# Scattering the transposed keys and queries over partitions in steps of three, in a scan-attention and mixture-of-experts kernel

## The chip, the cores and the metric

The kernel runs on one core of a Trainium2 chip. The time is the device time in microseconds (us) of one execution. Three runs of the kernel before took 1787.15, 1789.98 and 1791.46 us; the median is 1789.98 us. Durations of single instructions come from one profiled execution, which took 1786.6 us, of which 1784.6 us lie between its first and its last instruction (the span).

## The reference, cut to what matters

Four batches, eight heads, 768 time steps, 48 dimensions per head. A linear attention with a complex decay per key dimension, and on its output a layer of eight experts whose gates are balanced by eight rounds of row and column scaling.

```
for t in range(S):                                 # attention, per batch and head
    new_re = ar * S_re - ai * S_im
    new_im = ar * S_im + ai * S_re
    S_re, S_im = new_re + outer(k[t], v[t]), new_im
    y[t] = q[t] @ S_re                             # sums over the 48 key dimensions
x = y as [3072 tokens, 384]
P = exp(x @ w_gate - max), then 8 rounds of row and column scaling
for e in range(8):                                 # every expert on every token
    out += P[:, e:e+1] * (relu(x @ w1[e]) @ w2[e])
```

## The kernel before

The decay is turned into a running complex product z over time (`scan`), so that a block of time steps becomes matmuls: keys are divided by z (the tile `kh`, real and imaginary), queries are multiplied by it (in place in `zt`), and then scores, state and output are products over the key dimension. All matmuls of the experts run in fp32r with a high and a low part, so each product is three matmuls.

**First phase** (`phase1`, about the first 600 us). Twelve sub-blocks (`i` from 0 to 11) of 256 time steps each, three to a batch, each in two chunks of 128. For every sub-block: `load` (queries and keys, values), `norm` (decays, one sub-block ahead), `scan` and `post` on VectorE (DVE) with some steps on ScalarE (ACT), `attention`, `logits`, and, one sub-block later, the first two experts (`experts(i - 1)`), which are most of TensorE's (PE's) work. **Second phase** (`phase2a`, `phase2b`): the other six experts by a scheme that needs fewer products (15 for a 3 by 3 by 2 block), with weight sums prepared on VectorE, stored to DRAM (`w_d`) and fetched again for later blocks of tokens.

**Order of the work.** The program of the first phase is laid out by `Plan`: each step is a job with an engine, a cost, a rank, tiles that it reads and writes, and for a transfer the time `land` after which its result is expected (3.0 us for the transfers below, beside a cost of 0.68 us on SyncE's queue, SP). `order` runs the jobs through four in-order queues (PE, DVE, ACT, SP) and takes at each point the ready job of lowest rank; that order is then fixed in the program. The waits between engines are semaphores that the framework sets from which parts of a tile are written and read.

**The transfers in question** (lines 545 to 553). `scan` and `post` hold channels on 128 partitions: partition 8 d + h of channel third `ct` (0 to 2) is key dimension 16 ct + d of head h. The matmuls of attention want the key dimension on partitions and the head along the row. So twelve transfers per sub-block, from SBUF to SBUF, all issued from SP, re-lay them: `ks` (keys) and `qs` (queries) are tiles of 112 partitions, with real parts on rows 0 to 47 and imaginary ones on rows 64 to 111 (a = 0, 1; rows 48 to 63 stay zero). One transfer takes one third of the channels of one half: it reads 128 partitions and writes 16, in rows of 1 KB (two chunks; queries have one column more, the decay at the end, which `turn`, lines 616 to 619, copies to `rr` and `rn`). That is 6 transfers of 128 KB and 6 of 129 KB. In sub-block 0 (`i < THIRD`) the rank puts real and imaginary of a third side by side; in all others the three thirds of the real half go first.

**Who reads them.** PE: `keys` (line 574, transposes of `ks`), `scores` (line 588), `outs` (line 613). ACT: lines 617 and 618 (real column of `qs`), 619 (imaginary). DVE: line 649 (`sb`, for the new state), line 591 (masked scores). All depend on all of `ks` or all of `qs`. The experts' steps that run between them: lines 268 to 270 and 286 to 288 on PE, 274 on ACT, 278 on DVE (the low part `hl`).

**Memory.** Small constant tiles lie in the pool `cst`; the weights' pool `wp` comes directly behind it (ten tiles of 6144 bytes per partition, used in both phases), and the other pools of that side (`hp1`, `wx`, `wy`, `xp1`, later `hp2`, `ct`, `xc`, `xt`) behind `wp`. The tiles `qs`, `ks`, `zt`, `kh` and the second phase's X lie in pools allocated from the other end.

Of the kernel before, what the change touches and what calls it, by code (L numbers as in the profile page):

```python
# [6 lines left out]
F32 = mybir.dt.float32  # L7
# [13 lines left out]
NCH = SUB // CH  # L21
# [17 lines left out]
THIRD = 1  # L39
# [88 lines left out]
class Net:  # L128
# [9 lines left out]
    def build(self):  # L138
        tc, nc = self.tc, self.nc
        DR = bass.MemoryType.DRAM  # L140
        PS = bass.MemoryType.PSUM
        with ExitStack() as ctx:
            dram = ctx.enter_context(tc.tile_pool(name="dram", bufs=1, space=DR))
            cst = ctx.enter_context(tc.tile_pool(name="cst", bufs=1))
            self.wp = ctx.enter_context(tc.tile_pool(name="wp", bufs=WIDE))
            self.psA = ctx.enter_context(tc.tile_pool(name="psA", bufs=2, space=PS))

            self.ones = cst.tile([128, 128], F32, name="ones")
            nc.vector.memset(self.ones, 1.0)
            self.warm = cst.tile([128, 16], F32, name="warm")  # L150
            self.ident = cst.tile([128, 128], F32, name="ident")
            self.nident = cst.tile([128, 128], F32R, name="nident")
            self.mask = cst.tile([128, 4, CH], U8, name="mask")
            self.bm05 = cst.tile([128, 16], F32, name="bm05")
            nc.vector.memset(self.bm05, -0.5)
            self.bw = cst.tile([128, 16], F32, name="bw")
            nc.vector.memset(self.bw, -0.75 * 0.4995)
            self.wgs = cst.tile([128, NCT, 2 * E], F32R, name="wgs")
            self.two = cst.tile([2 * E, E], F32, name="two")
            self.wgr = cst.tile([128, NCT, E], F32, name="wgr")  # L160
            self.P = cst.tile([128, self.ntt, E], F32, name="P")

            ns = self.N // SUB
            self.fl = cst.tile([128, ns * (NCT * NCH + 2) + 2], F32, name="fl")
            self.ok = cst.tile([128, 9], F32, name="ok")
            self.oki = cst.tile([1, 1], mybir.dt.int32, name="oki")
            self.wt = {}
            self.x_d = [dram.tile([128, NS, 2, NCT, 2, CH], F32, name=f"x_d{u}") for u in range(self.N // UN)]
            self.ye_d = [[dram.tile([128, C], F32, name=f"ye_d{u}_{i}") for i in range(self.ntt) if u < 2 or i < NS * NCH] for u in range(E)]
            self.dram = dram  # L170

            with ExitStack() as c2, ExitStack() as cw, tc.manual_schedule(engines={mybir.EngineType.PE}):
                with ExitStack() as c1:
                    with ExitStack() as ca:
                        self.phase1(c1, ca)
                    self.phase2a(c2, cw)
                self.phase2b(c2, cw)
            flag = nc.values_load(self.oki[0:1, 0:1], min_val=0, max_val=1)
            with tc.If(flag < 1):
                with ExitStack() as c3:  # L180
                    self.general(c3)
# [345 lines left out]
    def attention(self, i):  # L527
        nc, V, A, job = self.nc, self.nc.vector, self.nc.scalar, self.plan.add
# [17 lines left out]
        for t, dst, src, w in (("ks", self.ks, kh, CH), ("qs", self.qs, zt, CH + 1)):  # L546
            for a in range(2):
                for ct in range(NCT):
                    p = 64 * a + 16 * ct
                    gs = range(ct * NCH, ct * NCH + NCH)  # L550
                    need = [("kh", a, g) for g in gs] + [("kr", a, g if i < THIRD else 0, k) for g in gs for k in range(TR)] if t == "ks" else [(*u, g) for u in (("z", s, a), ("ze", s)) for g in gs]
                    self.last = [job("SP", 0.68, lambda p=p, dst=dst, src=src, w=w, a=a, ct=ct: nc.sync.dma_start(dst[p:p + 16, :, :, :w], src[:, a, ct * NCH:ct * NCH + NCH, :w]),
                                     need, [(t, a, ct)], -3e6 + 40 * i + (2 * (t == "qs") + a + 4 * ct if i < THIRD else 6 * (t == "qs") + 3 * a + ct), land=3.0)]

        def chunk(c):
            ib = (i * NCH + c) % 2
# [845 lines left out]
```

## Time and profile before

| quantity | us |
|---|---|
| median of three runs | 1789.98 |
| profiled execution | 1786.6 |
| its span | 1784.6 |
| PE busy in the span | 1714.9 |
| DVE busy | 1285.6 |
| ACT busy | 805.2 |

A row of a table by stretches gives the stretch, then for PE, PE's weight loads (PEld), DVE, ACT and POOL the busy us with the count of instructions, then the granted clock of PE (1.00 is full speed), the mean busy share of the 16 DMA engines, and GB/s. In a list in time order a row is start, duration, engine, line, operation, output and inputs, and in brackets the idle time of the engine just before with what ended it. "Who waited for it" lists engine, line, idle us in total and how many times. The rows of transfers give their size in KB and the median us from issue to landing.

### The profile page before, as it was taken

How to read it: one execution, taken by the hardware profiler on the slowest of the kernel's cores; microseconds unless marked ns; L12 is line 12 of the kernel's file. 1: busy time of each engine (PE TensorE's matmuls, PEld its weight loads, DVE VectorE, ACT ScalarE, POOL GpSimd, SP SyncE). 2: the span in 40 equal slices, each digit the busy share in tenths (PEclk: the TensorE clock that was granted, in tenths of full speed). 3: DMA queues.
4: the chain of work that ended last, by engine and by line, in shares of the span. 5: the costliest groups of instructions: out<-in, count | busy, mean ns of one | idle time of the engine just before them, and what ended most of it. 6: DMA issues, size and time to landing. Idle time of an engine off the chain costs nothing.

```text
span 1784.6 us, 35158 instructions
## 1 busy us (share of the span) xinstructions
PE 1714.9 (96%) x13864; PEld 1664.0 (93%) x13864; DVE 1285.6 (72%) x2927; ACT 805.2 (45%) x1853; POOL 6.1 (0%) x13
## 2 busy tenths in 40 slices
PE   6899999999999889999999999999999999999998
PEld 3788899988898889999999999999999999999998
DVE  8788888888887468999884566766566765556564
ACT  7655555555554455565553433333333333333332
POOL 1000000000000000000000000000000000000000
PEclk9999999999999999999999999999999999999999
DMA  7455555555534675878896556576555657455561
GB/s 224 97 124 124 122 117 120 98 119 122 99 93 103 176 262 207 286 275 279 283 320 231 214 185 241 197 260 236 204 216 187 236 202 267 177 207 190 213 232 40
DMA packets 161422, 338.41 MB, mean 190 GB/s; under 512 B 13024, under 2 KB 120800, under 8 KB 161248
## 3 DMA queue, kind: packets, MB, share of 16 engines
q1 hardware_dynamic: 160448, 335.68, 59.0%
q8 instruction: 111, 1.82, 0.4%
q14 instruction: 63, 0.52, 0.1%
q10 hardware_dynamic: 800, 0.39, 0.1%
HBM read 236.07 MB, written 81.00 MB: 178 GB/s over the span
## 4 chain that ended last, share of the span: by engine, by line


## 5 line engine op out<-in xcount | busy, mean ns | idle before, releaser
L1137 ACT ACTIVATE hh<-s 128x384 fp32r<-128x384 f32 x384 | 201.9, 526 | 430.0 <-DVE s L1133 389.1
L1133 DVE TENSOR_TENSOR s<-s,A 128x384 f32<-128x384 f32 x316 | 174.4, 552 | 149.1 <-PE A L1119 145.6
L1042 PE MATMUL po<-w_d,hh 128*128 128x384 f32 x768 | 258.2, 336 | 0.0
L1041 PE MATMUL po<-w_d,hh 128*128 128x384 f32 x768 | 257.6, 335 | 0.0
L1043 PE MATMUL po<-w_d,hl 128*128 128x384 f32 x768 | 257.6, 335 | 0.0
L1144 DVE SCALAR_TENSOR_TENSOR hl<-s,hh 128x384 fp32r<-128x384 f32 x384 | 211.8, 552 | 6.2
L268 PE MATMUL ph<-xh,w 128*128 128x256 f32 x576 | 169.4, 294 | 1.6 <-ACT hf L274 1.2
L269 PE MATMUL ph<-xl,w 128*128 128x256 f32 x576 | 164.5, 286 | 0.0
L270 PE MATMUL ph<-xh,w 128*128 128x256 f32 x576 | 164.3, 285 | 0.0
L1130 ACT ACTIVATE s<-B 128x384 f32<-128x384 f32 x192 | 94.2, 491 | 121.9 <-PE B L1119 118.2
L1133 DVE TENSOR_TENSOR s<-s,B 128x384 f32<-128x384 f32 x189 | 104.1, 551 | 56.4 <-PE B L1119 54.3
L1042 PEld LDWEIGHTS po<-w_d,hh 128*128 128x128 f32 x768 | 144.3, 188 | 0.0
L1041 PEld LDWEIGHTS po<-w_d,hh 128*128 128x128 f32 x768 | 144.2, 188 | 0.0
L274 ACT ACTIVATE hh<-ph 128x256 fp32r<-128x256 f32 x192 | 73.5, 383 | 156.7 <-PE ph L270 153.6
L1043 PEld LDWEIGHTS po<-w_d,hl 128*128 128x128 f32 x768 | 144.2, 188 | 0.0
L286 PE MATMUL po<-w,hh 128*128 128x384 f32 x384 | 134.8, 351 | 0.4 <-ACT yst L294 0.4
L288 PE MATMUL po<-w,hl 128*128 128x384 f32 x384 | 131.7, 343 | 1.0 <-DVE hl L278 0.5
L287 PE MATMUL po<-w,hh 128*128 128x384 f32 x384 | 130.8, 341 | 0.0
L1042 PE MATMUL po<-w_c,hh 128*128 128x384 f32 x384 | 129.2, 336 | 0.0
L1041 PE MATMUL po<-w_c,hh 128*128 128x384 f32 x384 | 128.9, 336 | 0.0
L1043 PE MATMUL po<-w_c,hl 128*128 128x384 f32 x384 | 128.9, 336 | 0.0
L1152 DVE TENSOR_TENSOR s<-s,B 128x384 f32<-128x384 f32 x64 | 35.4, 554 | 119.2 <-PE B L1119 118.3
(248 smaller groups left out, 4109.6 us busy)
## 6 DMA issues: line engine op xcount, KB each, us to landing
w_d<-w_d SPq DMA_DIRECT2D x64, 768.0 KB, 7.2
w_a<-w_d SPq DMA_DIRECT2D x48, 768.0 KB, 4.3
w_b<-w_d SPq DMA_DIRECT2D x48, 768.0 KB, 5.7
w_c<-w_d SPq DMA_DIRECT2D x48, 768.0 KB, 6.5
raw<-in_w_dram SPq DMA_DIRECT2D x32, 576.0 KB, 5.3
w_d<-w_a SPq DMA_DIRECT2D x16, 768.0 KB, 3.3
w_d<-w_b SPq DMA_DIRECT2D x16, 768.0 KB, 4.7
w_d<-w_c SPq DMA_DIRECT2D x16, 768.0 KB, 6.1
```

The lines of the kernel that those rows point to most:

```text
L268: nc.tensor.matmul(p, w[:, 0, cs], xh[:, ct, :], start=(ct == 0), stop=False)
L269: nc.tensor.matmul(p, w[:, 0, cs], xl[:, ct, :], start=False, stop=False)
L270: nc.tensor.matmul(p, w[:, 1, cs], xh[:, ct, :], start=False, stop=(ct == NCT - 1))
L286: nc.tensor.matmul(o, hh[:, s], w2h, start=f == 0, stop=False)
L287: nc.tensor.matmul(o, hh[:, s], w2l, start=False, stop=False)
L288: nc.tensor.matmul(o, hl[:, s], w2h, start=False, stop=f == NF - 1)
L1041: nc.tensor.matmul(po[k], hh[:, s], w2[:, 0], start=c == 0, stop=False)
L1042: nc.tensor.matmul(po[k], hh[:, s], w2[:, 1], start=False, stop=False)
L1043: nc.tensor.matmul(po[k], hl[:, s], w2[:, 0], start=False, stop=c == NF - 1)
L1133: V.tensor_tensor(S[nm], S[nm], ps, op)
L1137: A.activation(hh, S[nm], AF.Relu)
L1144: V.scalar_tensor_tensor(hl, S[nm], 0.0, hh.bitcast(F32), ALU.max, ALU.subtract)
```

## The change

Three edits. A transfer of third `ct` starts at row 64 a + ct and writes every third row, so key dimension 16 ct + d goes to row 3 d + ct of its half in place of row 16 ct + d; keys and queries have the same new order, the 48 rows of a half are the same set. In sub-blocks 1 to 11 the rank puts real and imaginary transfers of one third in turn. A tile `gap` of 128 bytes per partition that nothing uses is put into `cst`, so that `wp`, and what lies behind it, begins 128 bytes later, at a multiple of 256 bytes.

```diff
             self.P = cst.tile([128, self.ntt, E], F32, name="P")
+            cst.tile([128, 32], F32, name="gap")
...
-                    p = 64 * a + 16 * ct
+                    p = 64 * a + ct
...
-                    self.last = [job("SP", 0.68, lambda p=p, dst=dst, src=src, w=w, a=a, ct=ct: nc.sync.dma_start(dst[p:p + 16, :, :, :w], src[:, a, ct * NCH:ct * NCH + NCH, :w]),
-                                     need, [(t, a, ct)], -3e6 + 40 * i + (2 * (t == "qs") + a + 4 * ct if i < THIRD else 6 * (t == "qs") + 3 * a + ct), land=3.0)]
+                    self.last = [job("SP", 0.68, lambda p=p, dst=dst, src=src, w=w, a=a, ct=ct: nc.sync.dma_start(dst[p:p + 3 * 15 + 1:3, :, :, :w], src[:, a, ct * NCH:ct * NCH + NCH, :w]),
+                                     need, [(t, a, ct)], -3e6 + 40 * i + (2 * (t == "qs") + a + 4 * ct if i < THIRD else 6 * (t == "qs") + 2 * ct + a), land=3.0)]
```

## The prediction

> **What bounds the kernel now.** I read the stages first (busy time per stretch of the span), then the idle time of TensorE and who caused it, then one sub-block closely on each queue, then the granted clock.
>
> ```profile
> span 1784.6 us, 35158 instructions
> PE 1714.9 (96%) x13864; PEld 1664.0 (93%) x13864; DVE 1285.6 (72%) x2927; ACT 805.2 (45%) x1853; POOL 6.1 (0%) x13
> ...
> core 0: us, PE busy (x) PEld busy (x) DVE busy (x) ACT busy (x) POOL busy (x), PEclk, DMA share, GB/s
> 450.00:500.00 50.00, 45.10 (x516) 42.64 (x516) 38.32 (x97) 25.49 (x70) 0.00 (x0) 0.93 0.52 107
> 1000.00:1200.00 200.00, 199.88 (x1138) 198.28 (x1137) 132.34 (x258) 71.20 (x141) 0.00 (x0) 1.00 0.60 220
> ```
>
> TensorE (PE) sets the time everywhere. In the second phase it is busy 199.88 of 200 us, so nothing that shortens a transfer or a VectorE step there can show. In the first phase (about the first 600 us, twelve sub-blocks of some 48 us) it is idle for several us in every 50, and its clock is at times below 1. The question is what those idle us wait for. The view of the line that issues the changed transfers, L552, answers it:
>
> ```profile
> L552 SPq DMA_DIRECT2D ks<-kh x72: 547/591/1305, 36.1 to 576.0; - x72
> L552 SPq DMA_DIRECT2D qs<-z x72: 547/597/1817, 37.6 to 579.9; - x72
> ...
>   DVE sb L649: 29.3, 11
>   ACT rn L619: 25.4, 12
>   PE s L588: 21.3, 11
> ...
>   PE s L574: 5.4, 7
> ...
> DMA to landing us min/median/max: 3.3/5.8/8.1
> ```
>
> Once per sub-block PE stands still for the queries (L588, the scores), 21.3 us in 11 waits, and seven times for the keys (L574), 5.4 us. VectorE and ScalarE stand still for the same transfers at the same time. So TensorE has no other work in its order while they travel, and this is on the path that sets the end. Sub-block 6, in time order on SP, PE, ACT and DVE:
>
> ```profile
> 327.09 3.79 SPq L552 DMA_DIRECT2D ks<-kh  x6
> 331.04 3.78 SPq L552 DMA_DIRECT2D qs<-z  x6
> ...
> 335.94 0.99 PE L574 MATMUL s<-ident,ks 112*128 112x112 f32 x8
> 342.31 1.33 PE L588 MATMUL s<-qs,ks 112*32 112x32 f32 x64 [2.25 <-DMA qs<-z]
> ...
> 339.27 0.22 ACT L617 ACTIVATE rr<-qs 48x8 f32<-48x8 f32 x1 [1.70 <-DMA qs<-z]
> 342.27 0.21 ACT L619 ACTIVATE rn<-qs 48x8 f32<-48x8 f32 x1 [2.56 <-DMA qs<-z]
> ...
> 342.29 0.56 DVE L649 TENSOR_TENSOR sb<-U,qs 48x384 f32<-48x384 f32 x1 [3.44 <-DMA qs<-z]
> ```
>
> The twelve transfers are issued within 7.7 us, 0.63 us apart (3.79 / 6). Yet the imaginary queries, which L619 reads, are there only at 342.27, 15.2 us after the first issue and some 7.5 us after the last one ended (331.04 + 3.78). The real ones (L617) were there at 339.27, 3.0 us earlier: the queue works them off one after another, slower than they are issued. PE arrived at 340.06 (342.31 - 2.25), 13.0 us after the first issue; VectorE at 338.85 (342.29 - 3.44), 11.8 us after. How fast the queue runs in that time:
>
> ```profile
> qs<-z SPq DMA_DIRECT2D x72, 129.0 KB, 7.1
> ks<-kh SPq DMA_DIRECT2D x72, 128.0 KB, 4.6
> ...
> 329.50:340.00 10.50, 10.49 (x133) 9.83 (x132) 9.04 (x26) 4.88 (x14) 0.00 (x0) 1.00 1.16 122
> 700.00:800.00 100.00, 99.99 (x570) 98.95 (x569) 92.90 (x253) 56.16 (x112) 0.00 (x0) 1.00 0.77 270
> ```
>
> The last two columns are the busy share of the DMA engines and what they moved. While the twelve travel, the engines are full (1.16, packets overlap) and move 122 GB/s, 105 per full share (122 / 1.16). In the second phase, where transfers write all 128 partitions, a full share is 351 GB/s (270 / 0.77). So it isn't the engines that are short, but what a transfer into 16 neighbouring partitions can take in.
>
> **The change part by part.** Step of three. It adds and removes no instruction: 144 transfers of the same bytes, and every consumer reads all 48 rows of a half, so a permutation of rows costs PE, ScalarE and VectorE nothing. What changes is the rate. The twelve hold 6 x 128 + 6 x 129 = 1542 KB, 1.58 MB; at 122 GB/s that is 12.9 us, and of the 15.2 us from first issue to use, 2.3 us are start and landing. For PE not to wait, the data may take 13.0 - 2.3 = 10.7 us, a rate of 148 GB/s; for VectorE not to wait, 11.8 - 2.3 = 9.5 us, 166 GB/s. The trace shows no destination with a step. The lower bound is the rate as it is, 122; the upper one is the issue, 129 KB in 0.63 us, about 208 GB/s, since 351 can't be fed. Between these I go by the spread of the destination: 16 rows give 105, 128 rows 351, so 46 rows, straight between them, about 171 GB/s (an estimate). That is above both thresholds: data 9.2 us, in use 11.5 us after the first issue, so PE's waits on queries and keys go: 21.3 + 5.4 = 26.7 us.
>
> [...]
>
> Order. Real and imaginary in turn adds nothing to issue. It lets the first imaginary keys go third or second where they went fourth, and SP might wait some tenths for VectorE to finish them; what is behind on SP (the queries, then stores of ye_d) isn't urgent, as the queue and not SP is late. In sub-block 0 the halves are issued in turn already:
>
> ```profile
> qs<-z SPq DMA_DIRECT2D x6, 129.0 KB, 5.6
> ```
>
> (the transfers by line in the first 50 us). 5.6 us there is better than the 7.1 of all, but those issues also lie further apart. I price the order alone at between 0 and the whole wait, and take 0, as the step already clears the thresholds. [...]
>
> Clock. When PE has stood still, its clock is halved for a while. These rows are the stretches of half clock after the waits, and one of full clock:
>
> ```profile
> 155.99:159.41 3.42, 3.42 (x15) 3.42 (x15) 1.79 (x5) 0.66 (x2) 0.00 (x0) 0.50 0.93 254
> 295.94:299.35 3.41, 3.41 (x15) 3.40 (x14) 2.69 (x8) 1.11 (x5) 0.00 (x0) 0.50 1.03 292
> 343.73:347.14 3.41, 3.41 (x14) 3.41 (x15) 2.97 (x8) 1.76 (x8) 0.00 (x0) 0.50 0.91 255
> 391.51:394.93 3.42, 3.36 (x69) 3.33 (x70) 2.72 (x5) 2.69 (x12) 0.00 (x0) 0.50 1.04 347
> 442.71:446.13 3.42, 3.42 (x17) 3.20 (x15) 2.48 (x8) 0.92 (x5) 0.00 (x0) 0.50 1.00 295
> 490.50:497.33 6.83, 4.62 (x39) 4.46 (x32) 4.13 (x13) 2.12 (x10) 0.00 (x0) 0.50 0.60 179
> 541.70:548.53 6.83, 6.16 (x77) 5.62 (x78) 4.46 (x11) 3.31 (x14) 0.00 (x0) 0.50 0.39 147
> 312.00:315.41 3.41, 3.41 (x24) 3.26 (x23) 3.38 (x7) 2.59 (x6) 0.00 (x0) 1.00 0.23 87
> ```
>
> 14 matmuls in 3.41 us against 24 at full clock. PE is busy 27.8 us in the seven rows together (3.42 + 3.41 + 3.41 + 3.36 + 3.42 + 4.62 + 6.16), half of which, 13.9 us, is lost to the clock. With the waits gone these should go. I keep back 3.4 us: two stretches of 3.4 us, half of each, for the two long rows, in which PE was also idle for other reasons.
>
> What is late next. VectorE is PE's partner in this phase:
>
> ```profile
> sum 480.00, PE 450.41 PEld 426.09 DVE 400.18 ACT 256.19 POOL 0.00; mean PE 45.04 PEld 42.61 DVE 40.02 ACT 25.62 POOL 0.00
> ...
> DVE hl L278 <- ACT hf L274: 34.1, 34, 2.7
> ```
>
> The first row is the sum of ten stretches of 48 us from 97 to 577, the second VectorE's longest waits from 50 to 640. Per sub-block VectorE works 40.0 us. PE works 45.0, of which 1.3 (13.9 / 11) is the clock, so 43.7: PE stays the longer one by 3.7 us, and VectorE's 34.1 us of waiting for PE's products (through ScalarE) is slack on PE's side. VectorE and ScalarE lose their own wait for the queries (29.3 and 25.4 us) with it. I keep back 1.2 us, 0.1 a sub-block, for new short waits of PE on VectorE.
>
> Gap. 128 bytes more ahead of the weights' pool: no instruction. It can only change the pace at which the pool's tiles are read or filled. Filling is hidden in the second phase (199.88 of 200). For reading, compare matmuls that stream from the pool with matmuls that stream from X, elsewhere, both 384 wide:
>
> ```profile
> L1041 PE MATMUL po<-w_d,hh 128*128 128x384 f32 x768 | 257.6, 335 | 0.0
> L1119 PE MATMUL B<-X,w_b 128*128 128x384 f32 x317 | 106.6, 336 | 0.0
> ```
>
> 335 and 336 ns: where the operand lies doesn't show. I take 0; rounding leaves half a ns either way, 7 us over 13,864 matmuls.
>
> The sum: 26.7 + 13.9 - 3.4 - 1.2 = 36.0 us off the profiled run's 1786.6 us (span 1784.6, 2.0 around it), so 1750.6. The median of the runs shown is 1789.98, 3.4 above the profiled run; from it, 1754.0.
>
> **The rivals.** VectorE binds. If the 34.1 us of waiting at L278 aren't slack but come back, VectorE can shed only its 29.3 us and PE waits at its products of hl: 1790 - 29 = 1761, worse if it waits for the later transfers too. For it: VectorE would be busy 40.0 of some 44 us, and the two are interlocked every 2 us. Against: those waits are VectorE waiting for PE, not the reverse.
>
> The rate doesn't move. If 122 GB/s is set by the reading side or by packets of 1 KB, the waits stay and so does the time, 1790. For it: in the same rows source and packets don't change either. Against: the reading side spans all 128 partitions, as in transfers that reach 351.
>
> The transfers wait for each other. The rows of the three thirds now interleave: each spans 46 rows that overlap the next one's span. If the semaphores are set by first and last row, the second third of a half waits on SP for the first to land, at least 3.3 us (the least of the landings above). Then keys go at 0, 3.3, 6.6 us (and 0.63 later each for the other half), queries at 7.9, 11.2, 14.5, the last at 15.1, landed at 18.4 in place of 15.2. PE loses 3.2 us in 11 sub-blocks, 35 us, and the clock falls in the four that were spared, 4 x 1.7: 1790 + 42 = 1832. It decides as soon as a transfer of the dozen waits over 2 us on SP. For it: alternating halves is what would soften such a wait. Against: nothing in the rows; before, thirds are disjoint either way and go back to back.
>
> **How the numbers follow.** Forecast 0.67: 1742 to 1766, from the full 40.6 us, less 7 us for the pool, to only the waits without the clock (1763) and 3 us of new ones. VectorE binding 0.16: 1757 to 1776. No change 0.08: 1787 to 1793. Transfers in a row 0.09: about 1832. A change under 0.2% (3.6 us) can't be told from none here. The range 1742 to 1776 takes in the first two cases, 0.83. Faster 0.83, same 0.08, slower 0.09.
>
> **What would show it.** Right: qs and ks land in a median under 5 and 4 us; the stretch after the first key issue moves over 150 GB/s; PE's waits at L588 and L574 for DMA fall from 26.7 us to under 5; half-clock stretches between 100 and 600 us nearly vanish; each sub-block is about 3.3 us shorter; 1000 to 1200 us looks as before. Wrong: waits of SP inside the dozen (transfers in a row), landings at 7.1 us as before (rate), or PE idle at L288 for hl (VectorE). A second phase with another pace per matmul would mean that the gap matters.

## The result, and the profile after

The changed kernel takes 1736.44 us (median of four runs, 1733.28 to 1737.60) against 1790.28 us: the ratio is 0.9699, 95% interval 0.9681 to 0.9717, so 53.8 us less. The forecast was 1754 us in a range from 1742 to 1776; the time lies 5.6 us under the range. In kernels with the gap, line numbers are one higher than before from line 162 on, since the gap is one line.

The head of the page after, then the queue of the transfers in the view of line L553 (before: L552):

```profile
span 1733.9 us, 35159 instructions
PE 1693.0 (98%) x13864; PEld 1642.9 (95%) x13864; DVE 1283.3 (74%) x2927; ACT 804.7 (46%) x1853; POOL 6.1 (0%) x13
...
  ACT rr L618: 11.8, 11
  DVE sb L650: 2.6, 4
  ACT rn L620: 0.6, 3
...
  PE s L575: 0.4, 1
DMA to landing us min/median/max: 2.9/4.1/5.2
...
qs<-z SPq DMA_DIRECT2D x72, 129.0 KB, 4.6
ks<-kh SPq DMA_DIRECT2D x72, 128.0 KB, 3.6
```

The same instructions, but PE's waits for queries and keys, 21.3 and 5.4 us, are down to 0.4; VectorE's 29.3 to 2.6. Queries land in 4.6 us in place of 7.1. Sub-block 6 again, on SP, PE, ACT and DVE:

```profile
309.40 3.80 SPq L553 DMA_DIRECT2D ks<-kh  x6
313.37 3.80 SPq L553 DMA_DIRECT2D qs<-z  x6
...
322.10 1.33 PE L589 MATMUL s<-qs,ks 112*32 112x32 f32 x64
...
320.64 0.22 ACT L618 ACTIVATE rr<-qs 48x8 f32<-48x8 f32 x1 [0.82 <-DMA qs<-z]
321.11 0.21 ACT L620 ACTIVATE rn<-qs 48x8 f32<-48x8 f32 x1
...
321.20 0.56 DVE L650 TENSOR_TENSOR sb<-U,qs 48x384 f32<-48x384 f32 x1
```

The dozen is issued as fast as before, so nothing waits on SP. PE comes to the scores 12.7 us after the first issue (322.10 - 309.40; before, it arrived after 13.0 us), but without a bracket: no wait. ScalarE finds the real queries 11.2 us after the first issue, and the imaginary ones are there with them; before, they came 3.0 us later.

Two more rows, of 480 us in the first phase and of the stretch from one and the same early product of the second phase (into the tile `F`) to the end of the span (for before, then for after):

```profile
97.00:577.00 480.00, 450.41 (x6072) 426.09 (x6071) 400.18 (x984) 256.19 (x700) 0.00 (x0) 0.97 0.53 113
668.40:1784.60 1116.20, 1110.20 (x6314) 1104.27 (x6314) 755.98 (x1623) 439.88 (x874) 0.00 (x0) 1.00 0.61 223
...
97.00:577.00 480.00, 472.73 (x6567) 447.73 (x6555) 416.26 (x1024) 270.08 (x745) 0.00 (x0) 1.00 0.50 127
626.90:1733.90 1107.00, 1100.80 (x6314) 1094.21 (x6314) 754.33 (x1623) 440.14 (x874) 0.00 (x0) 1.00 0.62 225
```

In the first phase PE gets through 6567 matmuls in place of 6072 and the clock is at 1.00 in place of 0.97. And the second phase, which the forecast took as untouched, is 9.2 us shorter for the same 6314 matmuls, though PE was busy in all but some 6 us of it before and is after, at the same clock. Of the span's 50.7 us, 41.5 fall ahead of that product (668.4 to 626.9) and 9.2 behind it. Ahead of it PE's busy time fell from 604.7 us (1714.9 - 1110.2) to 592.2 (1693.0 - 1100.8) for the same number of matmuls, and its idle time from 63.7 to 34.7: 12.5 us that go with the clock and 29.0 us of waits.

### The profile page after: what moved, and what is told of

The parts are those of the page before. It is cut to its first block, busy times and chain, and to the rows that moved or that the text cites. A ratio compares the mean times of both kernels' runs of the same rounds, so it can differ in the third digit from the quotient of the medians.

```text
span 1733.9 us, 35159 instructions
## 1 busy us (share of the span) xinstructions
PE 1693.0 (98%) x13864; PEld 1642.9 (95%) x13864; DVE 1283.3 (74%) x2927; ACT 804.7 (46%) x1853; POOL 6.1 (0%) x13
## 4 chain that ended last, share of the span: by engine, by line
## 5 line engine op out<-in xcount | busy, mean ns | idle before, releaser
L1043 PE MATMUL po<-w_d,hh 128*128 128x384 f32 x768 | 256.6, 334 | 0.0
L1042 PE MATMUL po<-w_d,hh 128*128 128x384 f32 x768 | 256.5, 334 | 0.0
L269 PE MATMUL ph<-xh,w 128*128 128x256 f32 x576 | 166.7, 289 | 1.6 <-ACT hf L275 1.2
L271 PE MATMUL ph<-xh,w 128*128 128x256 f32 x576 | 162.4, 282 | 0.0
L1042 PEld LDWEIGHTS po<-w_d,hh 128*128 128x128 f32 x768 | 144.2, 188 | 0.0
L1043 PEld LDWEIGHTS po<-w_d,hh 128*128 128x128 f32 x768 | 144.2, 188 | 0.0
L287 PE MATMUL po<-w,hh 128*128 128x384 f32 x384 | 133.0, 346 | 1.3 <-ACT yst L295 1.3
L288 PE MATMUL po<-w,hh 128*128 128x384 f32 x384 | 128.9, 336 | 0.0
L1043 PE MATMUL po<-w_c,hh 128*128 128x384 f32 x384 | 128.5, 335 | 0.0
L1042 PE MATMUL po<-w_c,hh 128*128 128x384 f32 x384 | 128.5, 335 | 0.0
```

The source lines that it names most:

```text
L269: nc.tensor.matmul(p, w[:, 0, cs], xh[:, ct, :], start=(ct == 0), stop=False)
L271: nc.tensor.matmul(p, w[:, 1, cs], xh[:, ct, :], start=False, stop=(ct == NCT - 1))
L287: nc.tensor.matmul(o, hh[:, s], w2h, start=f == 0, stop=False)
L288: nc.tensor.matmul(o, hh[:, s], w2l, start=False, stop=False)
L1042: nc.tensor.matmul(po[k], hh[:, s], w2[:, 0], start=c == 0, stop=False)
L1043: nc.tensor.matmul(po[k], hh[:, s], w2[:, 1], start=False, stop=False)
```

## The experiments

Four kernels took the change apart. They ran side by side on one chip, before at 1788.1 us.

**Gap alone** (e1_gap: before with `cst.tile([128, 32], F32, name="gap")`).

> The kernel before with only the 128 unused bytes ahead of the weights' pool. Theory A (the address of the pool sets the pace of the products of the second phase, L1117 to L1119): the second phase is 9 us shorter, as in the changed kernel (about 1107 against 1116 us), the first phase is unchanged, so about 1781 us, and the 48 us sub-blocks keep PE's waits of 26.7 us. Theory B (the second phase runs faster for another reason, such as the clock or the transfers that now come earlier): 1790 us, no change, and a 200 us stretch of the second phase holds 1138 to 1143 matmuls as before and not 1146 to 1155.

1778.49 us, 0.9948 of before (0.9930 to 0.9967): 9.3 us less by that ratio. PE's waits stay at 21.3 and 5.4 us. Theory A holds: 128 bytes that nothing uses are worth the second phase's whole gain.

**All but the gap** (e2_nogap: the changed kernel without that line).

> The changed kernel without the 128 bytes: step of three and real and imaginary in turn. Theory A: about 1745 us, 41 to 45 us under before, all of it in the first phase, and the second phase at its old pace. Theory B: about 1736 us, as the changed kernel.

1744.69 us, 0.9749 (0.9721 to 0.9778): 45 us less by the ratio, 43 by the medians. Theory A again; the two ratios multiply to 0.9698, the whole change.

**Step alone** (e3_step).

```diff
-                    p = 64 * a + 16 * ct
+                    p = 64 * a + ct
...
-dst[p:p + 16, :, :, :w]
+dst[p:p + 3 * 15 + 1:3, :, :, :w]
```

> The step of three alone, thirds of the real half first as before, no gap. Theory A (the step alone clears the thresholds, order is worth nothing): as e2_nogap, about 1745 us, last queries in use some 11.5 us after the first key issue, PE waits at L588 and L574 under 5 us. Theory C (most of the rate comes from working on the two halves at once): the last queries come 13 us or more after the first issue, VectorE still waits at L649, and the time lies between, 1755 to 1780 us.

1754.64 us, 0.9815 (0.9789 to 0.9840): 33 us less. Neither theory has it whole: the time is just under Theory C's range, and in sub-block 6 the last queries come 13.1 us after the first issue, as Theory C had it, but its cause, the work on both halves at once, is not what brings most (next run). In the view of the transfers' line:

```profile
  ACT rn L619: 19.4, 11
  DVE sb L649: 11.2, 11
  PE s L588: 6.3, 9
  ACT rr L617: 4.6, 6
```

The imaginary queries, read by L619, still come too late in all eleven sub-blocks, by a little, and PE waits for them in nine, 6.3 us in all. The step brings most, not all.

**Order alone** (e4_order: `3 * a + ct` to `2 * ct + a` in the rank).

> Real and imaginary in turn alone, 16 neighbouring rows as before, no gap. Theory A: no gain, 1785 to 1792 us, landings of 7 us for the queries. Theory C: the rate of the twelve transfers rises well over 150 GB/s and most of the first phase's gain is there, 1745 to 1760 us.

1789.45 us, 1.0003 (0.9990 to 1.0016): nothing, as Theory A had it. Queries still land in 7.0 us, and PE waits 21.1 us. So order is worth nothing without the step and some 10 us with it (e3 to e2, 1754.6 to 1744.7; their intervals lie apart). The rates in sub-block 6 while the dozen is under way, for order alone, step alone, and both (after):

```profile
333.00:343.00 10.00, 10.00 (x131) 9.57 (x131) 9.07 (x26) 4.39 (x12) 0.00 (x0) 1.00 1.16 123
...
314.50:323.50 9.00, 9.00 (x124) 8.70 (x123) 8.70 (x24) 4.82 (x14) 0.00 (x0) 1.00 1.12 151
...
311.80:319.80 8.00, 8.00 (x60) 7.97 (x59) 7.76 (x21) 4.37 (x12) 0.00 (x0) 1.00 1.09 172
```

123, 151 and 172 GB/s. The prediction's thresholds were 148 for PE and 166 for VectorE: step alone stands at the first and under the second, both together clear both, but VectorE's only just, as some 4 GB/s in that row are other transfers. In the traces the last packet of these twelve ends 14.1, 11.9 and 10.8 us after the first issue.

The others asked why the gap acts, and what sets the rate; beside e9_x, e7_behind, e8_wponly and e10_two, before was at 1787.38 us. In the program's memory map the weights begin at 128 past a multiple of 256 bytes before the change and at a multiple after it, and the X tiles on the other side at a multiple in both. The four X tiles of `xc` lie behind the weights' pool and move with it, as do `hh`, `hl`. These places are those of the program's allocation and stand in no view of the profile; what the runs show is what a move by 64 or 128 bytes does. That two places are to be compared modulo 256 was my assumption, and no run tests it; below, operands are alike or unlike in that sense. Distances between starts of matmuls, worked out from the trace, were 181 ns from L1117 to L1118 in most cases before and 173 after.

**X moved instead of the weights** (e9_x: before, and a pool of 128 unused bytes opened ahead of `xa` on its side).

```diff
+        px = c2.enter_context(tc.tile_pool(name="px", bufs=1, side="right"))
+        px.tile([128, 32], F32, name="px")
         xa = c2.enter_context(tc.tile_pool(name="xa", bufs=1, side="right"))
```

> The kernel before, with the weights' pool where it was (128 past a multiple of 256) and 128 unused bytes ahead of the pools of the other side in the second phase, so that the tiles X that L1117 to L1119 stream also begin 128 past a multiple of 256. Theory R (what counts is that the two operands of a product, the weights loaded and the tile streamed, begin at the same place modulo 256): the steps from L1117 to L1118 go from 181 to 173 ns as in e1_gap, about 1779 us. Theory P (what counts is that the weights' pool itself begins at a multiple of 256): as before, 1788 us.

1778.90 us, 0.9944 (0.9924 to 0.9964). Theory R: with the weights off the multiple and X off it too, the gain is as large as with the gap, and the step from L1117 to L1118 is 173 ns in most cases. So the gain goes with how the operands lie to each other (1778.90 us here, 1778.49 with the gap), not with the pool's own address.

**Only what lies behind the weights moved** (e7_behind: before, and a pool of 128 unused bytes opened right after `wp`).

> The kernel before, with 128 unused bytes behind the weights' pool: weights stay 128 past a multiple of 256, the hidden tiles hh and hl and the four X tiles behind the pool move to a multiple of 256. Theory R: the products L1041 to L1043, whose operands agreed, now disagree; with 8 ns for each of their 1152 triples and for the X tiles that agreed, the second phase is about 11 us longer, 1799 us. Theory P: 1788 us, as before.

1794.28 us, 1.0038 (1.0025 to 1.0051), 6.8 us more, where Theory R said 11 and Theory P none. The sign is R's; the price per product is under the 8 ns assumed, some 2 to 3 ns for the steps from L1041 to L1042 and from L1042 to L1043 (174 ns before, 176 and 177 here, means between 800 and 1600 us).

**Weights moved, what lies behind not** (e8_wponly: the gap, and 128 bytes more behind `wp`).

> The kernel before, with the weights' pool at a multiple of 256 and the pools behind it left 128 past one. Theory R: L1117 to L1119 get faster where X lies on the other side (8 us), L1041 to L1043 get slower by 8 ns a triple (9 us): about 1789 us. Theory P: 1778 us, as e1_gap.

One run, 1791.32 us: no gain, as Theory R had it, though the weights' pool begins at a multiple of 256.

**A smaller gap** (e11_gap64: `[128, 16]`, 64 bytes, before at 1787.05 us).

> The kernel before with 64 unused bytes in place of 128 ahead of the weights' pool: weights 192 past a multiple of 256, X of the other side at one, so they still differ, by 64. Theory R in its strict form (any difference modulo 256 costs): the stretch from 800 to 1600 us holds about 4557 products as before, 1788 us. Theory R with a coarser unit (only a difference of 128 costs): 4596 products, 1778 us. Theory P: as before.

One run, 1783.62 us, between the two forms. The sharpest measure of all these is how many matmuls PE gets through from 800 to 1600 us, at full clock and always busy. In this order: before, after, e1_gap, e9_x, e7_behind, e8_wponly, e11_gap64:

```profile
800.00:1600.00 800.00, 799.80 (x4557) 796.12 (x4556) 528.54 (x1095) 312.55 (x623) 0.00 (x0) 1.00 0.63 231
...
800.00:1600.00 800.00, 799.82 (x4596) 795.63 (x4595) 517.34 (x1045) 304.76 (x605) 0.00 (x0) 1.00 0.62 227
...
800.00:1600.00 800.00, 799.82 (x4595) 795.46 (x4594) 531.65 (x1102) 312.78 (x622) 0.00 (x0) 1.00 0.63 231
...
800.00:1600.00 800.00, 799.81 (x4596) 795.67 (x4595) 530.92 (x1100) 315.60 (x629) 0.00 (x0) 1.00 0.64 232
...
800.00:1600.00 800.00, 799.85 (x4535) 796.49 (x4534) 525.00 (x1084) 309.60 (x615) 0.00 (x0) 1.00 0.64 229
...
800.00:1600.00 800.00, 799.79 (x4546) 796.29 (x4545) 527.79 (x1093) 312.88 (x624) 0.00 (x0) 1.00 0.63 229
...
800.00:1600.00 800.00, 799.75 (x4577) 795.85 (x4576) 530.02 (x1097) 314.46 (x627) 0.00 (x0) 1.00 0.64 232
```

The first number in brackets is the count. All operands alike, whatever they are alike at: 4596. Some products unlike by 128: 4557 and 4546; more of them: 4535. Unlike by 64: 4577. The count is steady: four kernels with the addresses of before (before, e2_nogap, e3_step, e4_order) have 4556 or 4557.

Theory R isn't the whole account, though. If each product paid for its own two operands alone, e7_behind, in which the products that are unlike in before and those that are unlike in e8_wponly are unlike together, would lose 39 + 50 = 89 products against 4596; it loses 61. And the mean step from L1117 to L1118 is 182.1 ns in before and 179.3 in e7_behind, where the operands of L1117 lie to each other as before or, with X in `xc`, unlike where they were alike. So here a product's own two operands don't set its price alone; that the products next to it count too is my guess.

**Other rows** (e10_two: the changed kernel, with every second row for two thirds of a half and 16 neighbours for the last).

```diff
-                    p = 64 * a + ct
+                    p, st = (64 * a + ct, 2) if ct < 2 else (64 * a + 32, 1)
...
-dst[p:p + 3 * 15 + 1:3, :, :, :w]
+dst[p:p + 15 * st + 1:st, :, :, :w]
```

> The changed kernel with other rows: the first two thirds of a half go to every second row of rows 0 to 31, the last third to 16 neighbouring rows, 32 to 47; again the same 48 rows for keys and queries. Theory S (the rate grows with the partitions that a transfer spans: 31 and 16 in place of 46): slower than the step of three, under 145 GB/s, PE waits at L588's place again by 5 us and more, 1742 to 1760 us. [...]

1733.23 us, 0.9702 (0.9685 to 0.9719), as the changed kernel. Theory S falls: a shorter span of rows isn't slower. The landings, and the rate in sub-block 6:

```profile
qs<-z SPq DMA_DIRECT2D x72, 129.0 KB, 3.6
ks<-kh SPq DMA_DIRECT2D x72, 128.0 KB, 3.1
...
309.70:316.70 7.00, 7.00 (x55) 7.00 (x53) 6.79 (x17) 3.41 (x11) 0.00 (x0) 1.00 0.95 191
```

191 GB/s against 172: faster transfers than with the step of three. Why these rows take in more, no run shows.

**The two side by side** (e12_two, the rows of e10_two, and e13_after, the changed kernel; before at 1787.05 us).

> The rows of e10_two again, beside the changed kernel on the same chip. If its faster transfers (the last query packet 9.9 us after the first issue, against 10.9) still find a wait to remove, 1 to 4 us under the changed kernel; if every wait of PE that transfers could remove is gone in the changed kernel, the same within 0.2%.

> The changed kernel itself, for the comparison with e12_two: 0.970 of before.

1732.81 us, 0.9692 (0.9674 to 0.9709), and 1735.06 us, 0.9708 (0.9694 to 0.9721). The intervals overlap, so these medians don't show a difference of 2 us. The transfers land 0.9 and 0.6 us sooner (3.7 and 3.1 us against 4.6 and 3.7), and the traces point to a small gain: the first product of the second phase starts at 608.9 us in e12_two, 609.1 in e10_two and 608.9 in e14_x64 below, against 614.9 in e13_after and 613.7 in after. PE's matmuls wait under 1 us in all for the twelve in each of them, so what the faster transfers shorten is something else, and isn't shown.

**The opposite difference** (e14_x64: e10_two with 64 unused bytes ahead of `xa`, before at 1787.72 us).

> The rows of e10_two with the changed kernel's gap, and 64 unused bytes ahead of the other side's pools, so that X begins 192 past a multiple of 256 and the weights at one: the opposite difference to that of e11_gap64, where two intervals of each triple fell to 170 ns and the one into the triple rose to 181. Theory R in its strict form: any difference costs, so between 800 and 1600 us fewer products than the 4596 of the changed kernel, 1735 to 1745 us. Theory Q (a difference of a quarter can also gain, by its sign): more than 4596 products and under 1732 us.

1735.76 us, 0.9707 (0.9691 to 0.9723), and this row of the same stretch:

```profile
800.00:1600.00 800.00, 799.77 (x4577) 795.81 (x4576) 514.58 (x1038) 304.02 (x604) 0.00 (x0) 1.00 0.62 226
```

4577, as many as with the other sign. In both, some intervals within a triple fall to 169 or 170 ns and others rise to 181 or 182; the sum is worse than with operands alike. Theory Q falls: no difference tried beats operands that lie alike (4577 at best against 4596). Here too a product's own operands are not all that counts: the step from before's L1042 to its L1043 rises to 178.8 ns on average (173.5 in e10_two), though the operands of both lie alike and only the other side's pools, X among them, were moved.

## Why the prediction was wrong, point by point

**What bounds the kernel:** right. PE's order stood still for the twelve transfers, and the waits went as named.

**Step of three:** right in that every third row in place of 16 neighbours raises the rate (122 to 151 GB/s in sub-block 6); the rate was overrated, and the line that gave it was wrong. It was drawn through rates per full DMA share (105 and 351), so its 171 was one too, but it was held against thresholds in GB/s as moved (148 and 166). Per full share the runs give 135 alone (151 / 1.12) and 158 with the order (172 / 1.09). That 172 is close to 171 is luck: e10_two is faster with fewer rows spanned (191 GB/s), so the span isn't the measure. What is, no run shows.

**Order:** wrong. It said "take 0, as the step already clears the thresholds": alone the order is 0, but the step only reaches PE's threshold and misses VectorE's, and the order then adds 21 GB/s (151 to 172, 14%) and about 10 us. Why turns help only with the step wasn't tested. What the rows do show is that with neighbouring rows the turns leave the rate where it was (123 GB/s at a share of 1.16).

**Clock:** right. The half-clock stretches between 97 and 577 us are gone, and the row of that stretch reads 1.00 for 0.97; in e13_after, the same kernel again, one of 3.4 us is left (at 509.7). So of the 3.4 us kept back for stretches that would stay little or nothing was needed. The 1.2 us for new waits of PE on VectorE were of the right size: PE's idle time at the experts' third product rose by 1.9 us, most of it a wait for VectorE (before, then after, by the page):

```profile
L288 PE MATMUL po<-w,hl 128*128 128x384 f32 x384 | 131.7, 343 | 1.0 <-DVE hl L278 0.5
...
L289 PE MATMUL po<-w,hl 128*128 128x384 f32 x384 | 129.4, 337 | 2.9 <-DVE tb L463 1.6
```

The two terms without what was kept back, 26.7 + 13.9 = 40.6 us, lie in the interval of e2_nogap (39.7 to 49.9 us of 1788.1), and one by one they are near the 29.0 us of waits and 12.5 us at the clock that the profiles give.

**Gap:** this is the step that failed and put the time outside the range. "335 and 336 ns: where the operand lies doesn't show. I take 0". It is 9.3 us, more than the 7 us that the low end of the range allowed for it by rounding. Without the gap the time lies inside the range (e2_nogap, 1744.69 us). The comparison was of the wrong rows. L1119 is the third product of a triple; most of the cost was in L1117, the first. Its rows were there to be read, before and, as L1118, after:

```profile
L1117 PE MATMUL B<-X,w_b 128*128 128x384 f32 x317 | 109.7, 346 | 0.0
L1118 PE MATMUL B<-X,w_b 128*128 128x384 f32 x317 | 106.8, 337 | 0.0
L1119 PE MATMUL B<-X,w_b 128*128 128x384 f32 x317 | 106.6, 336 | 0.0
...
L1118 PE MATMUL B<-X,w_b 128*128 128x384 f32 x317 | 108.0, 341 | 0.0
L1119 PE MATMUL B<-X,w_b 128*128 128x384 f32 x317 | 106.1, 335 | 0.0
L1120 PE MATMUL B<-X,w_b 128*128 128x384 f32 x317 | 106.1, 335 | 0.0
```

The first of three was 9 to 10 ns longer than its fellows and is now 6 ns longer, so the rows alone would not have priced the gap. The starts of the matmuls do: between 800 and 1600 us the mean step from the first to the second product falls from 182.1 ns to 176.1 in e1_gap, some 4 of the 6.8 us that the 39 products are worth. And the reading was of the wrong thing: I asked whether a tile's place shows, when it is the places of two tiles to each other. L1041's operands, both in or behind the pool, agreed; L1117's didn't, but for the X tiles of `xc`. With the gap's 9.3 us in the sum, 1754.0 would have been 1744.7, which is still 8 us above the measured time. Of these, 4.6 us are what was kept back, while waits and clock together gave 41.5 us, over the 40.6 of the two terms. Another 1.9 us may be the start of the sum: in the next series the median of before is 1788.1.

**The rivals.** VectorE binding: no; in the changed kernel it still waits 29.2 us for PE's products at the low part `hl` (through ScalarE; 39.4 before, over the whole span). No change of rate: no. Transfers that wait for each other: no, six issues still take 3.80 us.

## What to carry to other kernels

When a matmul-bound stretch shows one product of a repeated group with a longer mean than its twins (here 346 ns against 337 and 336), compare the addresses of its two operands with those of the others before taking the pace for given. The longer mean is a hint, not a price. Moving either operand is quick to try, but it moves others too and can lose (e7_behind, 6.8 us); a count of matmuls in a busy stretch tells 0.2% from a single run (here 4557 from 4546). For re-layouts within SBUF compare the rate per full DMA share with that of transfers over all partitions (here 105 and 351 GB/s), work out the rate from which the waiting engine no longer waits (here 148 and 166), and try other written rows until it is passed (here 122, then 151, 172 and 191); beyond that, faster transfers bought no gain here that is clear of the noise (1732.81 against 1735.06 us). Price a wait with the clock it costs: here 12.5 us went with the clock beside 29.0 us of waits.

## What was not expected of the hardware

In this kernel, with one kind of fp32r products whose two operands mostly begin 128 bytes apart modulo 256 by the program's memory map, PE got through 39 of 4596 matmuls fewer in 800 us (0.8%) than with operands that all begin alike, and it made no difference at which of the two places both begin (e1_gap 4595, e9_x 4596). A difference of 64 cost half of that with either sign (4577 and 4577). Tiles were moved by 64 and 128 bytes only; that 256 is the period, and not more, is an assumption that no run tests. The price of a product doesn't rest on its own two operands alone (e7_behind loses 61 products where 89 would follow; e14_x64 has a step of 178.8 ns for 173.5 with operands that lie alike). The cause inside the chip is open: the runs show where it costs, not why.
